# Own steps for the differences of the last two groups' second-layer operands, and a new written order

## The chip, the cores and the metric

The kernel runs on one core of one Trainium2 chip. The time is device microseconds of one execution, from launch to end; three runs of the kernel before gave a median of 918.45 us. The profile is of one more execution, whose own time is given below.

## The reference, cut to what matters

Windowed attention of 4 batches of 8 heads (576 tokens, head size 64, window 128) gives 2304 rows of 512. Two feed-forward layers follow, each 512 to 2048 to 512, and both are computed in full f32 precision:

```
attn = softmax(scale * q @ k.T + bias, masked to the window) @ v
x = attn.transpose(0, 2, 1, 3).reshape(2304, 512)
g = s * relu(x @ w_in1) ** 2 + b;   x = g @ w_out1
h = relu(x @ w_in2);                out = (h * h) @ w_out2
```

## The kernel before

**Precision.** A f32 operand is split in a high part, which ScalarE (ACT) copies to the matmul's type, and a low part, which VectorE (DVE) forms as operand minus high part (`split`, `act_copy`, `dve_sub`). A product is three matmuls: high by high, high by low, low by high.

**Stages.** First attention (steps S, P, T, C, U, X of 40 units, D their loads), with the weights' preparation (l, a, b, c) and the first feed-forward layer of six token blocks beside it (L, G, H, M). Then 32 units of 128 pairs of hidden columns: 8 for the last three token blocks of the first feed-forward layer (group 0) and 8 each for the three groups of 768 tokens of the second one (groups 1 to 3). A unit k makes its hidden values with seven products in place of eight (steps p k.1 to p k.7), with copies m, u, v on ACT and sums j on DVE between them, and squares them (r). In groups 0 and 1 the result is split (h) and multiplied by the second weights directly (F).

**The second product of groups 2 and 3**, around which the change lies. Here the second weights are multiplied by seven products too, over all 8 units of the group: step `X n.e` is one of 56 products of group n. Its index e runs over seven kinds, eight units each: e 0 to 7 is kind 1, then kinds 2, 7, 6, 5, 4 and 3. Each product takes its weights from step `e n.e` (a DMA of 256 KB from a store in DRAM) and its left operand from step `g n.e`. Kinds 1, 2, 5 and 4 split a unit's result as it stands. Kind 7 (e 16 to 23) needs a11 - a21, kind 6 (e 24 to 31) needs a21 + a22 and then that minus a11, both in place, and kind 3 (e 48 to 55) needs a12 - a11 in place. Before, `second_operand` forms them on DVE directly ahead of the split, all in one step. The difference of kind 7 goes to one tile, `r_all` (temp u3). An operand's halves lie in a ring of 6 (group 2) or 10 (group 3) places.

**What sets the order.** `ORDER` is a written list of steps. `InOrder` keeps every engine's instructions in the order in which the steps issue them; there is no scheduler. Each engine works its own list off and waits only on semaphores. All DMAs stand in one queue of SyncE (SP): weights (w, e), stores of prepared weights and sums (d, t, x), inputs (Y), outputs (O), and a DMA that must wait holds all behind it. `CHOICE` says for some steps which of DVE (v) and GpSimd (POOL, g) adds, `UNIT_ENGINES` which of ACT and DVE normalises and copies in an attention unit. Steps of the list in the order of the text: `C n.m.t` copies a bank of a finished kind, `O n.m.t` adds two kinds and stores a part of the output, `R k.i` and `t k.i` split and store sums of second weights that `N k.i` adds, `V` and `T` split and subtract inputs of a group that `Y` loads.

All instructions are recorded at line 29 (the helper), so the names of tiles tell them apart: `q` is a bank of a second product, `px` and `py` those of a unit, `m2...` a place in the weights' memory, `yw...` and `yr` results of units, `sh` and `sl` the one ring place that has tiles of its own.

Of the kernel before, what the change touches and what calls it, by code (L numbers as in the profile page):

```python
# [18 lines left out]
class InOrder:  # L19
# [24 lines left out]
    H13 c21 L15 c20 M12 c22 C10 U10 G14 a23 H14 X10 l30 G15 M13 L16 S11 M14 b23 L17 G16 P11 D13 L18 T11 H15 c23 M15 H16
    C11 G17 l32 a30 G18 U11 H17 X11 H18 L19 G19 b30 L20 S12 M16 L21 k0.1 a32 l31 M17 M18 P12 T12 a31 H19 G20 c30 C12 H20
    L22 l33 G21 b32 U12 X12 L23 G22 H21 S13 L24 M19 a33 b31 M20 M21 H22 P13 l34 b33 T13 G23 C13 c31 a34 M22 H23 U13 L25
    c33 G24 G25 c32 L26 k3.0 D14 L27 H24 M23 H25 X13 D15 S14 G26 G27 M24 l35 b34 L28 L29 P14 k4.1 T14 M25 H26 a35 C14
    H27 c34 k4.0 G29 b35 U14 M26 D16 X14 G28 H28 S15 L30 c35 P15 M27 M28 T15 C15 D17 G30 L31 H29 G31 U15 X15 L32 S16 M29
    H30 H31 D18 G32 L33 P16 T16 M30 D19 C16 H32 G33 M31 M32 H33 S17 U16 L34 P17 T17 X16 G34 C17 M33 L35 H34 S18 U17 M34
    G35 X17 H35 P18 L36 D20 T18 G36 C18 M35 D21 S19 U18 L37 H36 P19 T19 X18 M36 C19 S20 D22 U19 G37 L38 H37 P20 M37 T20  # L50
    G38 X19 C20 L39 S21 U20 H38 G39 H39 L40 P21 M38 G40 L41 M39 D23 H40 T21 G41 L42 X20 H41 C21 k6.0 S22 U21 M40 k0.0
    P22 T22 X21 C22 M41 S23 U22 G42 D24 H42 k7.0 k1.1 L43 P23 T23 X22 M42 C23 S24 G43 H43 k3.1 U23 P24 L44 T24 D25 D26
    C24 X23 M43 k1.0 G44 H44 L45 G45 S25 U24 L46 D27 M44 k5.0 X24 P25 T25 H45 G46 k2.1 C25 H46 D28 L47 n0.0 n0.1 S26 U25
    n0.2 P26 M45 n0.3 G47 n0.4 L48 T26 n0.5 X25 H47 n1.0 k2.0 M46 f0.0 C26 n1.1 G48 M47 n1.3 S27 f0.1 L49 n1.2 H48 E21
    P27 n1.4 D29 U26 T27 n1.5 n2.3 W21 G49 L50 E20 W20 n2.2 X26 C27 S28 U27 n2.1 f1.0 f1.1 n2.0 n2.4 H49 E22 E23 M48
    n2.5 W23 G50 P28 D30 n3.1 n3.0 W22 X27 n3.3 L51 T28 f2.0 f2.1 H50 M49 M50 n3.2 l0.3 n3.4 C28 S29 U28 l0.1 G51 H51
    n3.5 L52 n4.3 P29 T29 G52 k7.1 C29 l0.0 k6.1 X28 f3.0 D31 H52 L53 a0.1 S30 U29 n4.0 n4.1 l0.2 M51 a0.3 G53 f3.1 n4.2
    X29 k5.1 P30 L54 n4.4 n4.5 T30 n5.2 n5.3 a0.0 M52 b0.3 H53 D32 C30 b0.0 x0.3 S31 U30 G54 L55 b0.1 H54 X30 P31 S0.0
    D33 M53 T31 S0.1 c0.0 d0.0 G55 f4.0 D34 L56 c0.1 a0.2 l1.0 H55 f4.1 C31 U31 S32 n5.0 n5.4 b0.2 X31 n5.1 G56 M54 c0.2
    S33 P32 P33 d0.1 n5.5 M55 n6.1 x0.2 T32 d0.2 f5.0 L57 H56 T33 D35 C32 n6.3 U32 S34 n6.0 a1.0 c0.3 G57 C33 n6.2 X32  # L60
    c0.4 H57 l1.1 L58 d0.3 f5.1 U33 S35 X33 M56 P34 P35 n6.4 T34 T35 a1.1 M57 l1.2 c0.5 G58 d0.4 n6.5 C34 U34 b1.0 D36
    l1.3 f6.1 b1.1 n7.1 a1.2 H58 X34 S1.0 C35 L59 U35 S36 S1.1 D37 b1.2 G59 w1.4 L60 X35 M58 P36 T36 H59 c1.0 w2.4 c1.1
    a1.3 S37 D38 d1.0 d1.1 n7.0 D39 f6.0 d0.5 G60 C36 M59 S38 U36 P37 T37 H60 L61 c1.2 d1.2 b1.3 C37 w0.2 S39 P38 T38
    c1.3 d1.3 X36 G61 C38 L62 U38 P39 w2.0 T39 x1.3 c1.4 x1.2 X38 n7.2 n7.3 H61 U37 M60 d1.4 C39 c1.5 X37 U39 d1.5 G62
    X39 Q Y0.0 Y0.1 L63 n7.4 Y0.3 n7.5 M61 w0.0 Y0.2 w0.1 f7.1 H62 f7.0 G63 M62 V0.1 T0.1 H63 T0.2 w0.4 V0.5 M63 E40
    T0.3 p0.1 V0.2 V0.6 p0.2 w0.3 V0.7 m0 p0.6 u0 w1.0 w1.1 j0.0 p0.7 T0.4 r0.0 V0.4 p0.5 v0 h0.0 E41 W40 V0.3 p0.4 j0.2
    w0.5 w1.2 W41 F0.0 F0.2 j0.1 w1.3 w2.2 r0.2 F0.3 p1.1 m1 r0.1 p0.3 p1.6 w2.1 h0.2 j0.3 F0.1 u1 F0.4 h0.1 p1.2 E42
    p1.7 v1 F0.6 j1.0 F0.9 r0.3 p1.5 E43 W43 F0.5 j1.1 w2.5 r1.1 F0.7 p1.4 w1.5 F0.10 r1.0 h0.3 F0.8 F0.11 w4.3 p1.3
    h1.1 j1.2 w2.3 l2.0 F0.12 j1.3 w3.1 p2.1 p2.2 m2 p2.6 h1.0 F1.2 F1.0 u2 F0.14 p2.7 w4.0 j2.0 r1.2 F0.13 v2 p2.5 r1.3
    r2.0 h1.2 F1.3 j2.1 w3.0 r2.1 F1.10 F1.1 p2.4 F1.8 p2.3 j2.2 F1.6 h1.3 F0.15 j2.3 F1.11 w3.3 p3.1 h2.1 m3 p3.2 r2.3  # L70
    w3.2 F1.12 F1.15 h2.0 p3.6 j3.0 p3.5 r2.2 Y1.3 a2.0 F1.7 w4.2 r3.0 u3 h2.2 w4.1 F2.2 h2.3 F1.9 l2.1 p3.7 v3 a2.1
    F2.8 Y1.2 F1.4 p3.4 F1.5 F2.3 b2.0 j3.1 j3.2 F1.13 p3.3 b2.1 j3.3 l2.2 F2.0 F2.6 r3.3 p4.1 r3.2 p4.2 F2.1 F1.14 m4
    p4.6 r3.1 F2.9 F2.10 h3.1 h3.0 u4 p4.7 j4.0 w5.0 p4.5 w3.5 F2.13 F2.4 F2.5 w6.1 F2.11 w4.5 v4 p4.4 S2.0 F2.12 S2.1
    w5.2 h3.2 F2.14 F2.7 c2.1 j4.1 h3.3 c2.0 j4.2 p4.3 p5.1 F3.10 w6.0 j4.3 r4.1 r4.3 w5.3 w3.4 r4.0 F2.15 w5.1 F3.0
    F3.1 m5 d2.1 r4.2 a2.2 F3.9 d2.0 p5.6 h4.0 F3.2 F3.3 u5 p5.2 b2.2 h4.2 w4.4 j5.0 w7.0 F3.14 p5.7 h4.1 F3.11 F3.8
    w7.3 c2.3 v5 p5.4 c2.2 p5.5 j5.2 w6.2 j5.1 r5.2 l2.3 F3.12 x2.2 F3.6 a2.3 h4.3 r5.1 p5.3 F3.7 d2.3 F4.2 F4.8 Y1.0
    b2.3 F3.4 F4.10 j5.3 r5.3 F3.13 F3.15 F4.14 F3.5 h5.2 h5.1 p6.1 F4.9 h5.3 w5.4 p6.2 c2.5 F4.3 W42 F4.12 F4.0 m6 Y1.1
    r5.0 p6.6 h5.0 F4.1 F4.6 u6 j6.0 w5.5 F4.11 w7.1 d2.2 F4.4 w8.0 w6.3 p6.7 F4.13 p6.5 w9.0 F4.7 F4.5 v6 F5.2 j6.1
# [1195 lines left out]
```

## Time and profile before

| | before |
|---|---|
| runs | 918.18, 918.45, 919.23 us |
| profiled execution, its own time | 916.52 us |
| its span, first to last instruction | 914.7 us |
| TensorE (PE) busy | 878.5 us, 96% |
| weight load (PEld) busy | 787.4 us, 86% |
| DVE, ACT, POOL busy | 663.4, 536.7, 167.7 us |
| DMA | 216.83 MB, 70.0% of 16 engines' span |
| granted TensorE clock | 0.996 |

PE is the busy engine nearly everywhere, so what a change is worth is read from the places where PE stands idle: the start, the end of attention, and the second products of groups 2 and 3. In a window's row the first number is its length, then come the busy times of PE, PEld, DVE, ACT and POOL with their instruction counts, the granted clock, the DMA engines' mean busy share and GB/s. A timeline's row has start, length, engine, line, operation, tiles, shapes, the number of instructions merged, and in brackets how long the engine had been idle and what released it.

### The profile page before, as it was taken

The page shows a single profiled execution, that of the slowest core. Times are in us where ns is not written, and L with a number is a line of the kernel's source. Part 1 is how long each engine was busy: PE and PEld are TensorE (multiplying, and loading weights), DVE is VectorE, ACT ScalarE, POOL GpSimd, SP SyncE. Part 2 cuts the span into 40 slices and gives each one's busy share as a digit, 9 for nine tenths or more (in the row PEclk, how much of TensorE's full clock was granted, in tenths as well). Part 3 has the DMA queues.
Part 4 walks back from the last instruction along what each step waited for, and adds up shares of the span by engine and source line. Part 5 has one row for each costly group of instructions (what it writes and reads, how often), then busy time and mean ns, then how long its engine had stood idle before and what let it go on. Part 6 is the DMA issues. An engine that isn't in the chain of part 4 may idle for free.

```text
span 914.7 us, 16299 instructions
## 1 busy us (share of the span) xinstructions
PE 878.5 (96%) x5680; PEld 787.4 (86%) x5680; DVE 663.4 (73%) x1504; ACT 536.7 (59%) x1227; POOL 167.7 (18%) x242
## 2 busy tenths in 40 slices
...
GB/s 344 174 190 99 201 112 195 47 70 219 103 100 242 313 248 271 307 305 316 226 287 355 262 229 198 306 294 261 319 336 349 327 282 252 292 265 229 187 271 98
DMA packets 131378, 216.83 MB, mean 237 GB/s; under 512 B 15840, under 2 KB 74208, under 8 KB 131296
## 3 DMA queue, kind: packets, MB, share of 16 engines
q1 hardware_dynamic: 131296, 215.79, 70.0%
...
## 4 chain that ended last, share of the span: by engine, by line
PE 81%; DVE 9%; ACT 4%; DMA 3%; issue 2%; SPq 1%; POOL 0%; ACTq 0%; DVEq 0%
PE ha L29 14%; PE po L29 14%; PE px L29 13%; PE oa L29 12%; PE py L29 10%; PE q L29 8%; PE s L29 7%; PE u L29 2%; DMA m2wol<-wd 1%; DVE ywoh L29 1%; DVE st L29 1%; DVE m2woh L29 1%; DVE pr_t L29 1%; DMA yf<-xd 1%; DMA st<-w_out 1%
## 5 line engine op out<-in xcount | busy, mean ns | idle before, releaser
L29 POOL TENSOR_TENSOR st<-st 128x256 int32<-128x256 int32 (+1 forms) x123 | 87.2, 729 | 363.8 <-DVE st L29 251.0
L29 ACT ACTIVATE pr<-pr,nd 128x256 f32<-128x256 f32 (+1 forms) x125 | 57.9, 474 | 49.5 <-DVE nd L29 49.5
L29 ACT ACTIVATE st<-st 128x512 int32<-128x512 uint32 (+3 forms) x74 | 62.4, 859 | 5.6 <-DVE st L29 3.4
L29 DVE SCALAR_TENSOR_TENSOR r_all<-r_all,s_sb 128x256 f32<-128x256 f32 (+1 forms) x64 | 43.0, 675 | 24.4 <-ACT r_all L29 23.8
L29 ACT ACTIVATE tr<-tr 128x384 f32<-128x384 f32 x48 | 25.2, 525 | 55.4 <-DVE tr L29 55.3
L29 PE MATMUL oa<-ga,woh 128*128 128x256 f32 x256 | 48.2, 287 | 0.0
L29 ACT ACTIVATE r_all<-ha 128x256 f32<-128x256 f32 (+1 forms) x64 | 31.0, 486 | 24.7 <-PE ha L29 19.2
L29 DVE SCALAR_TENSOR_TENSOR st<-st 128x512 int32<-128x512 int32 (+1 forms) x42 | 37.3, 890 | 11.0 <-ACT st L29 10.4
L29 PEld LDWEIGHTS oa<-ga,woh 128*128 128x128 f32 x256 | 39.7, 191 | 2.2 <-issue 1.8
L29 DVE CUSTOM_DVE_ANT_0 pr<-s,bases 128x256 f32<-128x256 f32 (+1 forms) x96 | 31.7, 385 | 11.3 <-PE s L29 11.3
L29 PE MATMUL ha<-x0h,wih 128*128 128x256 f32 x128 | 38.4, 300 | 0.0
L29 PE MATMUL ha<-x0l,wih 128*128 128x256 f32 x128 | 36.6, 286 | 0.0
L29 PE MATMUL ha<-x0h,wil 128*128 128x256 f32 x128 | 36.6, 286 | 0.0
L29 PE MATMUL oa<-ga,wol 128*128 128x256 f32 x128 | 36.2, 283 | 0.0
L29 POOL TENSOR_TENSOR sph<-wih,wil 128x256 f32<-128x256 f32 x17 | 13.5, 814 | 117.7 <-PE ha L29 117.2
L29 ACT ACTIVATE r_all<-px 128x384 f32<-128x384 f32 x32 | 15.7, 490 | 29.5 <-PE px L29 29.4
L29 PE MATMUL s<-raw 64*128 64x256 f32 (+1 forms) x224 | 30.5, 388 | 0.8 <-DVE x0l L29 0.8
L29 DVE TENSOR_SCALAR st<-st 128x512 int32<-128x512 int32 (+2 forms) x52 | 26.2, 507 | 5.9 <-ACT st L29 5.1
L29 POOL TENSOR_TENSOR sph<-sph 128x256 f32<-128x256 f32 x26 | 22.6, 888 | 33.7 <-DVE spl L29 20.9
L29 PE MATMUL px<-m2xl,m2wil 128*128 128x384 f32 x138 | 27.9, 337 | 0.0
L29 PEld LDWEIGHTS ha<-x0h,wih 128*128 128x128 f32 x128 | 24.9, 195 | 3.5 <-issue 2.5
L29 PE MATMUL ha<-x2h,wih 128*128 128x512 f32 x64 | 26.4, 412 | 0.0
...
## 6 DMA issues: line engine op xcount, KB each, us to landing
...
```

What stands on the lines that cost most here:

```text
L29: ins = op(*args, **kw)
```

## The change

The differences leave `second_operand` and become steps of their own, `q n.e`; the split stays in `g n.e`. Kind 7 now has two tiles in turn, u3 and u4. The written order is new from one end to the other, and so are `CHOICE` and `UNIT_ENGINES`. No product, split or transfer is added or left out. By the two programs POOL has 220 additions in place of 207, DVE 644 in place of 653.

```diff
-    def second_operand(n, e):
+    def parts_of(n, e):
         m, y = SECOND[e // NP], e % NP
         a11, a22, a12, a21 = (result_of(n * NP + y, c) for c in range(4))
+        return m, a11, a22, a12, a21, {1: a11, 2: a12, 7: temp(f"u{3 + y % 2}"), 6: a11, 5: a21, 4: a22, 3: a12}[m]
+
+    def second_difference(n, e):
+        m, a11, a22, a12, a21, src = parts_of(n, e)
         tt = vector.tensor_tensor
-        src = {1: a11, 2: a12, 7: temp("u3"), 6: a11, 5: a21, 4: a22, 3: a12}[m]
         if m == 7:
             tt(src, a11, a21, ALU.subtract)
         elif m == 6:
...
             tt(a11, a21, a11, ALU.subtract)
         elif m == 3:
             tt(a12, a12, a11, ALU.subtract)
-        split(*operand_halves(n, e), src, act_copy, dve_sub)
+
+    def second_operand(n, e):
+        split(*operand_halves(n, e), parts_of(n, e)[-1], act_copy, dve_sub)
...
-            table.update({f"{x}{n}.{e}": lambda y=y, n=n, e=e: y(n, e) for x, y in (("e", load_second), ("g", second_operand), ("X", second_product))})
+            table.update({f"{x}{n}.{e}": lambda y=y, n=n, e=e: y(n, e) for x, y in (("e", load_second), ("q", second_difference), ("g", second_operand), ("X", second_product))})
...
-    N1.1:v N2.1:v N3.0:v N3.1:v N7.1:v S0.1:g S1.1:g S2.0:g S3.0:g S3.1:g S4.0:g b0.0:vg b2.2:vg b3.0:vg b3.1:vg
+    N0.1:v N2.1:v N5.1:v N7.1:v S0.0:g S0.1:g S1.0:g S1.1:g S2.0:g S2.1:g S3.0:g S3.1:g S5.1:g b2.1:vg b2.2:vg
...
+    e2.14 t7.1 e2.15 t7.3 j23.2 t6.3 C2.1.1 r23.2 X2.10 g2.14 g2.13 X2.11 e2.16 g2.16 e2.18 X2.12 X2.13 e2.17 q2.17
```

**DVE in group 2, before.** These rows run from the difference of g2.20 to the low half of g2.25. `r_all` is kind 7's difference, `ywih2`, `ywil2` and others are results of units, and a row that writes `m2...` is the low half of a split.

```order
L29 TENSOR_TENSOR r_all_121<-ywoh0_7286 128x384
L29 TENSOR_TENSOR m2wil1_4703<-r_all_121,m2wil1_4703 128x384
L29 TENSOR_TENSOR ob220_7857<-q220_7699,k2m_7798 128x512
L29 TENSOR_TENSOR r_all_121<-ywol2_7370 128x384
L29 TENSOR_TENSOR m2woh1_4705<-r_all_121,m2woh1_4705 128x384
L29 TENSOR_TENSOR ywih2_7004<-ywih2_7004 128x384 x2
L29 TENSOR_TENSOR m2wih1_4433<-ywih2_7004,m2wih1_4433 128x384
L29 TENSOR_TENSOR r_all_121<-ywol2_7370,ywoh3_7518 128x384
L29 TENSOR_TENSOR m2woh1_4705<-r_all_121,m2woh1_4705 128x384
L29 TENSOR_TENSOR ywil2_7100<-ywil2_7100 128x384
L29 TENSOR_TENSOR ywih2_7004<-ywil2_7100,ywih2_7004 128x384
L29 TENSOR_TENSOR m2wil1_4703<-ywih2_7004,m2wil1_4703 128x384
```

**The same engine and place after**, from the difference q2.19 to the difference q2.22.

```order
L29 TENSOR_TENSOR tu4_7361<-ywoh2_7199,ywoh0_7290 128x384
L29 TENSOR_TENSOR ywih2_6975<-ywih2_6975 128x384 x2
L29 TENSOR_TENSOR m2wih1_4466<-r_all_121,m2wih1_4466 128x384
L29 TENSOR_TENSOR m2wil1_4684<-tu4_7361,m2wil1_4684 128x384
L29 TENSOR_TENSOR r_all_121<-ywoh0_7290 128x384
L29 TENSOR_TENSOR ywoh2_7199<-ywoh2_7199,ywil2_7109 128x384
L29 TENSOR_TENSOR ywil2_7109<-ywoh2_7199,ywil2_7109 128x384
L29 TENSOR_TENSOR m2wil1_4684<-r_all_121,m2wil1_4684 128x384
L29 TENSOR_TENSOR tu4_7361<-ywol2_7347 128x384
L29 TENSOR_TENSOR r_all_121<-ywol2_7347,ywoh3_7527 128x384
```

Before, every low half follows its own difference; now other operands' differences and halves stand between the two, and two tiles hold the differences of kind 7.

**SP in group 2, before.** The loads `m2...<-we` or `<-wd` bring weights of single products (`we22` is that of X2.21, `we41` that of X2.27), `we63<-` is the store t6.3, `out<-` the output stores of O2.2.

```order
L29 DMA m2wol0_4322<-we72_216 128x512
L29 DMA m2wol0_4322<-we62_212 128x512
L29 DMA m2wol1_4678<-we61_211 128x512
L29 DMA m2wol0_4322<-we42_204 128x512
L29 DMA m2wih1_4433<-we32_200 128x512
L29 DMA m2wih3_4650<-we51_207 128x512
L29 DMA m2xl1_4718<-we21_195 128x512
L29 DMA m2wil0_4688<-we12_192 128x512
L29 DMA m2wih1_4433<-we22_196 128x512
L29 DMA m2xl0_4675<-we71_215 128x512
L29 DMA out<-ob222_7850 128x256
L29 DMA we63_213<-m2wil3_4690 128x512
```

**The same queue and place after.**

```order
L29 DMA we63_213<-m2wil3_4698 128x512
L29 DMA m2wol0_4322<-we72_216 128x512
L29 DMA m2wol0_4322<-we52_208 128x512
L29 DMA m2wol0_4322<-we62_212 128x512
L29 DMA m2wol0_4322<-we42_204 128x512
L29 DMA m2wih1_4466<-we22_196 128x512
L29 DMA m2wih1_4466<-we32_200 128x512
L29 DMA m2wih3_4669<-we51_207 128x512
```

The load of X2.21's weights (`we22`) was the ninth, counted from that of X2.16 (`we72`); now it is the fifth. The store t6.3 stands ahead of them and no longer behind an output store.

**SP in group 3, before.** `out<-ob32` are the output stores of O3.2, `we51` the weights of X3.29.

```order
L29 DMA m2wol1_4678<-we62_212 128x512
L29 DMA m2wih3_4650<-we01_187 128x512
L29 DMA m2wil3_4690<-we11_191 128x512
L29 DMA out<-ob320_9148 64x256 x4
L29 DMA out<-ob322_9154 128x256
L29 DMA m2wol0_4322<-we51_207 128x512
L29 DMA m2xl1_4718<-we31_199 128x512
L29 DMA m2wih1_4433<-we00_186 128x512
```

**The same queue and place after.**

```order
L29 DMA m2wil0_4650<-we42_204 128x512
L29 DMA m2wol0_4322<-we41_203 128x512
L29 DMA m2wol0_4322<-we51_207 128x512
L29 DMA m2wol0_4322<-we61_211 128x512
L29 DMA m2wih1_4466<-we00_186 128x512
L29 DMA m2wol1_4693<-we62_212 128x512
L29 DMA out<-ob322_9191 128x256
L29 DMA out<-ob320_9194 64x256 x4
```

The loads for X3.27 to X3.29, X3.31 and X3.32 (`we31` too, further up) stood behind the output stores and now stand ahead of them.

## Rows read from the trace of the kernel before

**Rows 1.** Windows by stage: length, busy PE, PEld, DVE, ACT, POOL, clock, DMA share.
```profile
330.00:412.00 82.00, 76.31 (x474) 61.15 (x473) 65.87 (x169) 57.20 (x143) 21.38 (x39) 1.00 0.88 295
412.00:700.00 288.00, 286.59 (x1544) 264.70 (x1543) 208.86 (x373) 161.86 (x328) 53.12 (x68) 1.00 0.82 287
...
713.40:770.00 56.60, 52.36 (x390) 49.96 (x390) 45.13 (x90) 28.05 (x63) 4.80 (x5) 1.00 0.87 295
770.00:854.40 84.40, 84.40 (x564) 84.40 (x563) 54.89 (x109) 43.08 (x91) 0.00 (x0) 1.00 0.77 252
854.40:882.00 27.60, 24.17 (x188) 22.83 (x188) 19.86 (x40) 9.57 (x20) 0.00 (x0) 1.00 0.66 213
```

**Rows 2.** Timeline of PE: first steps and ends of the two stretches.
```profile
713.05 0.51 PE L29 MATMUL py<-m2xh,m2wol 128*128 128x384 f32 x2
713.39 1.23 PE L29 MATMUL q<-m2wol,m2wih 128*128 128x256 f32 x9
714.46 0.40 PE L29 MATMUL q<-m2wol,m2wil 128*128 128x256 f32 x2
...
767.99 0.52 PE L29 MATMUL q<-m2wil,m2wih 128*128 128x256 f32 x3
...
854.41 1.23 PE L29 MATMUL q<-m2wol,m2wil 128*128 128x256 f32 x9
...
889.87 0.52 PE L29 MATMUL q<-m2wol,m2wil 128*128 128x256 f32 x3
```

**Rows 3.** Waits of PE from 713.4 to 770: total, times, longest.
```profile
PE q L29 <- ACT m2wih L29: 1.8, 1, 1.8
PE q L29 <- ACT m2wil L29: 1.1, 2, 0.6
PE q L29 <- DMA m2wol<-wd: 0.8, 1, 0.8
```

**Rows 4.** Waits of PE from 854.4 to 914.
```profile
PE q L29 <- ACT m2woh L29: 2.3, 2, 1.5
PE q L29 <- ACT m2wil L29: 0.9, 1, 0.9
```

**Rows 5.** Timeline of DVE, ACT, PE around g2.26, and of DVE at 758.
```profile
749.84 0.55 DVE L29 TENSOR_TENSOR ywoh<-ywoh,ywil 128x384 f32<-128x384 f32 x1
...
751.10 0.52 ACT L29 ACTIVATE m2wil<-ywil 128x384 fp32r<-128x384 f32 x1 [1.77 <-DVE ywil L29]
...
751.67 1.57 PE L29 MATMUL q<-m2wih,m2wil 128*128 128x256 f32 x8 [0.60 <-ACT m2wil L29]
752.13 1.14 DVE L29 TENSOR_TENSOR ywoh<-ywoh,ywoh 128x384 f32<-128x384 f32 x2
...
758.33 0.55 DVE L29 TENSOR_TENSOR m2wil<-ywih,m2wil 128x384 fp32r<-128x384 f32 x1
758.80 0.55 DVE L29 TENSOR_TENSOR m2woh<-ywil,m2woh 128x384 fp32r<-128x384 f32 x1
```

**Rows 6.** Timeline of SP and PE: the load for X2.21, and X2.21.
```profile
738.44 0.43 SPq L29 DMA_DIRECT2D m2wih<-we  x1
...
743.17 0.56 DVE L29 TENSOR_TENSOR m2woh<-r_all,m2woh 128x384 fp32r<-128x384 f32 x1 [0.67 <-ACT m2woh L29]
...
745.45 1.31 PE L29 MATMUL q<-m2wih,m2woh 128*128 128x256 f32 x9 [1.82 <-ACT m2wih L29]
```

**Rows 7.** That load alone, asked by its tile: time to landing.
```profile
DMA to landing us min/median/max: 6.9/6.9/6.9
```

**Rows 8.** Timeline of SP: the output stores of O3.2.
```profile
869.75 3.09 SPq L29 DMA_DIRECT2D out<-ob  x5
```

**Rows 9.** Timeline of ACT and PE at the end of attention.
```profile
403.82 0.85 ACT L29 ACTIVATE m2xl<-yf 128x768 fp32r<-128x768 f32 x1 [1.62 <-DMA yf<-xd]
```

**Rows 10.** Waits of PE from 330 to 412.
```profile
PE oa L29 <- DVE ga_63l L29: 2.3, 1, 2.3
```

**Rows 11.** Timeline of POOL from 357 to 368.
```profile
358.20 5.59 POOL L29 TENSOR_TENSOR ewih<-ewih 128x256 int32<-128x256 int32 x5 [4.85 <-DVE ewih L29]
```

More of the change, by code (lines that the diff above doesn't have):

```diff
@@ L44 @@
[L44 to L78, printed above, removed]
@@ new lines @@
+    C12 U12 G20 L22 H19 G21 M19 l33 H20 X12 H21 L23 S13 G22 L24 M20 a33 b31 M21 P13 T13 H22 G23 M22 k2.0 b33 C13 c31 U13
+    L25 H23 X13 G24 L26 M23 l34 c32 G25 a34 D14 H24 H25 b34 l35 L27 c33 G26 S14 L28 G27 P14 M24 L29 T14 k4.0 a35 H26
+    k5.0 M25 c34 D15 C14 G28 b35 U14 H27 X14 L30 S15 M26 G29 H28 c35 D16 H29 D17 P15 G30 M27 M28 L31 T15 k6.0 H30 M29
+    C15 G31 H31 U15 X15 L32 G32 S16 L33 M30 D18 P16 H32 G33 M31 L34 D19 T16 M32 C16 S17 U16 H33 D20 G34 L35 P17 T17 H34
+    M33 C17 k4.1 X16 G35 H35 S18 U17 P18 M34 L36 T18 M35 k7.0 k3.1 G36 C18 L37 X17 H36 S19 U18 M36 D21 P19 T19 G37 L38
@@ new lines @@
+    c0.4 d0.3 f5.1 H57 L58 U33 S35 X33 P34 P35 M56 T34 T35 d0.4 a1.1 c0.5 G58 l1.2 C34 D36 M57 U34 L59 n6.4 l1.3 n6.5
+    f6.1 b1.0 H58 b1.1 X34 n7.1 S1.0 S1.1 C35 D37 a1.2 n7.0 U35 S36 b1.2 G59 w1.4 X35 w2.4 L60 D38 M58 P36 c1.0 H59 T36
+    a1.3 c1.1 G60 d1.0 S37 b1.3 M59 d1.1 D39 f6.0 n7.3 C36 U36 S38 P37 T37 H60 c1.2 L61 d0.5 C37 S39 d1.2 P38 T38 c1.3
+    w0.2 G61 C38 d1.3 L62 w2.0 X36 P39 x1.3 U38 T39 H61 x1.2 c1.4 X38 G62 U37 d1.4 X37 c1.5 C39 M60 d1.5 U39 L63 X39 Q
+    n7.2 H62 Y0.0 M61 Y0.1 G63 n7.4 Y0.3 w0.0 n7.5 M62 Y0.2 w0.1 f7.0 f7.1 V0.1 H63 w0.4 w0.3 T0.1 T0.2 T0.3 M63 V0.5
@@ new lines @@
+    h2.0 w5.2 p3.6 w3.3 F1.9 p3.2 F1.3 r2.2 r2.3 u3 h2.2 F1.14 r2.1 Y1.0 p3.7 w3.5 w5.1 h2.1 F1.6 F2.11 F1.13 j3.0 F2.0
+    a2.1 l2.2 F1.8 p3.5 h2.3 v3 F2.1 p3.4 j3.1 j3.2 F1.7 r3.1 F2.10 p4.1 m4 F1.12 r3.0 F2.2 p4.6 p3.3 b2.1 S2.0 h3.1
+    w3.4 S2.1 F2.3 j3.3 r3.3 F2.4 w4.4 u4 F2.8 W43 F2.5 c2.1 r3.2 c2.0 F2.15 h3.2 p4.7 F2.9 a2.2 w6.1 w6.2 v4 F2.13 p4.2
+    d2.1 w4.5 F2.14 h3.0 j4.0 F2.6 p4.4 j4.2 w7.3 p4.5 r4.2 j4.1 F2.12 F2.7 r4.0 h4.2 F3.0 F3.10 p4.3 F3.2 h3.3 p5.1
+    d2.0 F3.14 h4.0 j4.3 w5.3 r4.1 l2.3 p5.2 Y1.1 c2.3 m5 h4.1 F3.9 p5.6 F3.11 F3.8 F3.3 d2.3 u5 p5.7 r4.3 j5.0 w6.0
@@ new lines @@
+    j7.0 T1.3 F6.0 V1.2 p7.7 v7 w6.5 r7.0 l3.2 F6.6 p7.5 w8.3 p7.4 j7.1 T1.4 w8.1 h6.3 r7.1 w8.4 w8.2 V1.7 F6.11 p7.3
+    j7.2 F6.15 F6.9 p8.1 F6.8 F6.7 w7.4 w9.1 V1.5 F6.1 j7.3 a3.1 F6.12 m8 F6.13 p8.6 F6.10 r7.2 w8.5 F6.4 r7.3 F6.5 b3.1
+    V1.4 u8 p8.7 S3.0 p8.2 h7.0 h7.1 F7.0 w7.5 h7.2 F6.14 F7.1 j8.0 v8 F7.4 F7.2 h7.3 F7.3 F7.6 p8.4 a3.2 F7.5 p8.5
+    w10.0 V1.3 b3.2 S3.1 E80 w10.1 w9.3 r8.0 F7.7 Y2.1 j8.2 E81 j8.1 r8.2 w9.0 W80 F7.9 p9.1 F7.11 Y2.3 F7.8 m9 p8.3
+    r8.1 w9.4 F7.12 h8.1 W81 j8.3 E60 p9.6 F7.15 F7.13 p9.2 Y2.2 W60 h8.0 h8.2 F7.10 w10.3 c3.0 u9 x3.2 r8.3 c3.1 p9.7
@@ new lines @@
+    p11.4 l5.1 l5.0 d4.0 F9.8 b4.3 F10.1 F10.2 j11.2 p12.1 F10.0 x4.3 j11.0 d3.5 a5.1 d3.2 c4.5 p11.5 a5.0 F10.5 b5.1
+    m12 b5.0 j11.1 S5.0 F10.9 p11.3 F10.10 S5.1 l5.2 F10.6 j11.3 F10.11 r11.0 c5.3 c5.2 r11.2 h11.0 c5.1 p12.6 d4.1 u12
+    r11.3 F10.8 c5.0 r11.1 F11.0 l5.3 a5.2 p12.7 p12.2 h11.2 v12 p12.4 l6.1 F11.2 b5.2 F11.6 j12.2 j12.0 F10.7 h11.1
+    d4.4 a5.3 F11.4 r12.2 r12.0 p12.5 b5.3 x5.2 j12.1 r12.1 F11.3 F11.5 c5.4 F11.1 h12.2 F11.8 d4.5 h12.0 F11.7 p13.1
+    h11.3 d5.0 a6.1 F11.11 c5.5 x5.3 T2.1 h12.1 b6.1 m13 p12.3 j12.3 F12.2 p13.6 p13.2 l6.0 F11.9 T2.2 d5.1 F12.5 r12.3
@@ new lines @@
+    F12.1 a6.0 u13 l6.2 h12.3 F12.0 b6.0 d5.5 j13.0 F12.11 S6.0 S6.1 a6.2 p13.7 v13 c6.3 F12.6 p13.5 c6.2 F11.10 d5.4
+    d3.1 b6.2 j13.1 r13.1 c6.0 d5.3 p13.4 F12.7 c6.1 p13.3 r13.0 l6.3 j13.2 F12.3 c6.4 h13.0 F12.9 F12.4 j13.3 F13.0
+    p14.1 F12.8 x6.2 T2.3 h13.1 F12.10 F13.5 a6.3 r13.3 d6.3 d6.0 r13.2 l7.0 m14 b6.3 h13.2 F13.4 h13.3 l7.1 p14.2 a7.0
+    p14.6 c6.5 F13.1 F13.11 u14 b7.0 F13.2 a7.1 b7.1 j14.0 d6.4 F13.3 p14.7 F13.9 v14 p14.5 F13.10 x6.3 Y3.1 S7.0 j14.1
+    p14.4 S7.1 r14.1 p14.3 d6.1 c7.2 F13.8 c7.1 W62 c7.0 F13.6 j14.2 p15.1 j14.3 d5.2 d4.3 r14.0 l7.2 r14.2 h14.1 c7.3
@@ new lines @@
+    h14.0 d6.5 p15.2 d7.1 F13.7 l7.3 a7.2 m15 j15.0 F14.4 p15.6 y0.4 u15 b7.2 r14.3 F14.3 p15.5 d7.0 h14.2 F14.2 h14.3
+    V2.1 d7.3 a7.3 F14.1 d6.2 V2.2 p15.7 c7.4 x7.2 d7.2 F14.5 F14.11 b7.3 v15 W63 d7.4 j15.1 p15.4 x7.3 p15.3 j15.2
+    r15.1 j15.3 r15.0 y0.5 Y3.2 p16.1 p16.2 r15.2 F14.7 w19.0 r15.3 c7.5 h15.1 F14.10 F15.5 h15.3 F15.4 F15.11 V2.7 N0.0
+    F14.8 d7.5 V2.3 R0.0 O1.5 N0.1 F14.9 h15.0 F15.3 F15.9 Y3.3 R0.1 V2.6 F15.10 t0.1 t0.0 F15.1 R0.2 m16 p17.2 O1.4
+    O1.3 t0.2 T2.4 p17.1 R0.3 h15.2 j16.0 y1.4 p16.6 y1.5 F15.7 w20.0 u16 F15.2 p16.7 V2.5 p16.5 t0.3 V2.4 Y3.0 N1.0 v16
@@ new lines @@
+    j16.1 O1.1 p16.4 j16.2 m17 j17.0 F14.0 p16.3 j16.3 p17.6 p18.2 w19.2 R1.1 N1.1 r16.0 w19.3 u17 R1.3 p18.1 R1.2 R1.0
+    p17.7 w19.1 p17.5 F14.6 t1.1 F15.8 y2.4 v17 m18 y2.5 T3.1 t1.0 y3.4 j17.1 j18.0 p17.3 w20.2 w20.1 p18.6 t1.3 j17.3
+    r16.1 u18 r17.0 p17.4 O1.2 r18.0 p18.7 p19.1 j17.2 t1.2 v18 N2.0 N2.1 R2.1 p18.5 p19.2 R2.0 m19 y3.5 r16.3 t2.0
+    F15.0 j18.1 p19.6 R2.2 j19.0 r17.3 F15.6 R2.3 w22.0 p18.3 w21.0 g2.0 p18.4 j18.3 p19.5 t2.1 r17.2 w20.3 N3.0 u19
+    r18.1 R3.0 t2.2 p19.7 t2.3 R3.1 j18.2 N3.1 y4.4 t3.0 y4.5 v19 j19.1 p20.1 t3.1 m20 T3.3 R3.2 p19.4 w21.1 p20.2 R3.3
@@ new lines @@
+    j20.0 t3.2 w21.2 r17.1 j19.2 O1.0 p19.3 y5.4 r18.3 N4.0 r20.0 p20.6 j19.3 p21.1 p21.2 r16.2 u20 p20.7 r19.3 g2.2 m21
+    v20 j21.0 r19.1 p20.5 w22.2 w21.3 j20.1 g2.1 w22.1 N4.1 p20.4 R4.1 p20.3 p21.6 R4.2 j20.2 p22.1 R4.0 w23.0 t4.1
+    j20.3 r18.2 p21.5 r21.0 r19.0 y5.5 u21 R4.3 N5.0 p21.7 p22.2 r19.2 v21 m22 r20.2 j21.1 t3.3 t4.3 j22.0 p21.4 j21.2
+    r20.1 r22.0 w23.2 w22.3 r20.3 p21.3 e2.1 t4.0 p22.6 j21.3 e2.0 p22.5 e2.2 e2.4 p23.2 r21.2 N5.1 g2.5 g2.4 u22 w23.1
+    y6.4 g2.3 p22.7 p23.1 R5.3 R5.1 V3.2 v22 R5.0 y6.5 t5.0 t4.2 j22.1 r21.3 p22.4 T3.2 R5.2 p22.3 m23 e2.3 V3.1 e2.7
@@ new lines @@
+    q2.24 g2.18 g2.19 q2.20 q2.26 g2.20 t7.0 q2.21 e2.23 q2.22 e2.24 X2.17 e2.30 r23.3 r23.1 e2.29 q2.28 X2.18 g2.21
+    X2.19 e2.27 e2.28 m24 g2.22 X2.20 e2.32 X2.21 q2.50 g2.25 g2.24 C2.1.0 e2.34 e2.33 X2.22 q2.23 q2.27 g2.26 O2.2.2
+    g2.28 g2.27 X2.24 X2.25 e2.39 q2.29 O2.2.0 X2.26 g2.32 g2.23 X2.27 g2.33 X2.28 X2.23 e2.35 q2.31 g2.34 X2.32 e2.36
+    X2.33 e2.31 e2.42 g2.29 X2.29 q2.30 e2.47 X2.34 q2.55 g2.30 q2.48 C2.7.0 g2.35 C2.7.1 e2.40 e2.37 X2.30 X2.35 g2.31
+    X2.31 g2.39 e2.38 e2.46 e2.41 g2.36 p24.6 g2.41 e2.43 e2.45 V3.5 g2.37 X2.36 w27.0 X2.37 V3.7 g2.40 g2.38 g2.42
```

139 lines of the change are left out of this document (63 added, 76 removed).

## The prediction

> **What bounds the kernel now.** I read the windows by stage first, because PE is busy 878.5 of 914.7 us and a change can only win where PE is not fed. [Rows 1] show the reader four kinds of stretch. From 412 to 700 us PE lacks 1.41 of 288 us, and from 770 to 854.4 us nothing at all: PE and PEld are both busy 84.40 of 84.40. Three stretches lack something: the end of attention (82 less 76.31, 5.7 us), the second product of group 2 from 713.4 to 770 (56.6 less 52.36, 4.24 us), and that of group 3 from 854.4 to 882 (3.43 us). The clock is 1.00 in all five, so nothing here is owed to it. In group 2 the DMA engines are at 0.87, which will limit what can be had there.
>
> Busy time hides part of the loss, so I counted products instead, from the timeline of PE [rows 2]. The first product of group 2 begins at 713.39 and the next at 714.46: 1.07 us for one that is fed. Up to 767.99, 54.60 us later, stand 36 products and 8 steps of units with six matmuls each, at 0.17 us a matmul (two of them from 713.05 to 713.39). That is 36 x 1.07 + 8 x 1.02 = 38.5 + 8.2 = 46.7 us, so 7.9 us are lost. In group 3, 28 products lie between 854.41 and 889.87: 35.46 less 30.0 leaves 5.5 us lost.
>
> Here the Trainium skill has a rule ("Perfetto Trace Analysis", section "Identifying the Most-Contended Engine"): busy time of matmuls is a poor measure, the share of time in which weights are loaded a better one. By it the two stretches lack 56.6 less 49.96 and 27.6 less 22.83, that is 6.6 and 4.8 us, where PE's own busy time gives 4.2 and 3.4; the trace agrees with the skill in the stretch that is fully fed, where PEld too is 84.40. A sum held to PE's idle time alone could not pass 7.7 us for both, by the rule it could pass 11.
>
> Then I read who ends PE's waits there. In group 2 they are [rows 3] 1.8 us for `m2wih`, twice `m2wil` (1.1 together) and 0.8 us for a load; in group 3 [rows 4] twice `m2woh` (2.3, the longer 1.5) and 0.9 for `m2wil`. All but one name ACT, but two of them are something else, as the timeline tells. X2.21 starts at 745.45 after 1.82 us of waiting, while its operand's low half begins at 743.17 and takes 0.56; its weights were issued by SP at 738.44 [rows 6] and took 6.9 us to land [rows 7], so at 745.3. This wait is a load's. In group 3 the 0.8 us left beside the 1.5 of `m2woh` are X3.28's, whose load stands in SP's queue behind the five output stores that hold it from 869.75 for 3.09 us [rows 8].
>
> **The change, group 2.** No work is added or removed, the 48 differences (64 instructions) only leave the splits and are issued earlier. What that is worth is seen around g2.26 [rows 5]: its first difference runs at 749.84, ACT's copy only starts at 751.10 after 1.77 us on DVE, PE is released at 751.67 after 0.60, and DVE's next work starts at 752.13. So a kind-6 operand holds DVE 749.84 to 752.13 = 2.29 us, while unchained ones follow each other in 0.47 (758.33 to 758.80), and three of these are 1.41. Eight such save 8 x 0.88 = 7.0 us of DVE. A kind-7 low half also waits 0.67 for its copy [rows 6]: eight save 5.4. With two tiles for kind 7, a difference need not wait for the previous low half. These 12.4 us of DVE lie in a stretch of 56.6 us in which DVE is busy 45.13 and so idle 11.5: the waits on the chain are the idle time, and with them gone DVE has about its idle time as lead. X2.21's load goes from the ninth to the fifth place, so its 1.8 is taken too. What stays of the 7.9 us: the load wait of 0.8, and some 1.7 of short ones without a row, which makes 2.5 and a gain of 5.4.
>
> What is late next is the transfers. At share 0.87, the 54.60 us move 47.5 us' worth of full DMA. Were 0.88, the highest of [rows 1], a ceiling, the stretch would need 54.0 us and the gain be 0.6; at 1.00 it would need 47.5 and the bound be 7.1. Part of these transfers can wait for the next stretch (0.77). I take 1.0 us off the 5.4 for loads that land late and keep 4.4; the bounds are 0.6 and 7.1.
>
> **Group 3.** Of the 5.5 us, 2.4 are chained operands (0.9 and 1.5), 0.8 the load behind the stores. DVE has 7.7 us idle (27.6 less 19.86), DMA only 0.66. The stores now follow the loads, and the differences are issued ahead of the splits. I leave 1.2 us for waits that remain: gain 4.3. Bounds: the waits named, 3.2, and all, 5.5.
>
> **End of attention.** S1.0's two additions move from DVE to POOL ahead of b1.2's and of P36's memset, for which T36's transposes wait. Five such additions took 5.59 us [rows 11], so 1.1 each: between 0 and 2.2 us late, and I take 0.7 as the cost, since POOL is busy only 21.38 of 82. It is nearer to the lower end because the memset is not needed as soon as it is issued. M63's wait of 2.3 on H63's low half [rows 10] goes, since H63 is issued earlier. But the products behind it need V0.2's high half, which ACT starts at 403.82 after waiting 1.62 for a load [rows 9], and the load chain is not moved. So I give 0 for it; its bounds are 0 and 2.3.
>
> **The rest** of the order (units' steps F, r, h, weights w, attention) is new as well. PE lacks only 1.41 us from 412 to 700, so at best 1.4 can be won. I take 0, with the loss bounded in the second rival.
>
> **Sum:** 4.4 + 4.3 - 0.7 = 8.0 us from the profiled execution's own 916.52 (span 914.7, 1.8 around it) gives 908.5. That execution is 1.93 below the median of the runs, 918.45, so the forecast against the median is 910.4 us. Its bounds are 0.6 + 3.2 - 2.2 = 1.6 and 7.1 + 5.5 + 2.3 + 1.4 = 16.3, that is 916.9 and 902.2; its own likely range is 906 to 913.
>
> **Rivals.** *First: transfers bind group 2.* At the ceiling of 0.88 its gain is 0.6, group 3 still gives 4.3 and attention takes 0.7: 4.2 us, so 914.3 (range 913 to 916.5). For it: 0.87 in the stretch, a landing of 6.9 us, a wait for a load in [rows 3]. Against it: the stretches on both sides run lower, 0.82 and 0.77, so loads can move.
>
> *Second: the new order makes short waits in the stage of units,* where PE has no slack to give: sums, copies and splits of one unit are written next to products of another, and a step that comes a little late costs PE directly. At 0.5 us a wait (rather less than the 0.6 of [rows 3]) 16 of them, one for each unit of groups 0 and 1, take back all 8.0: 918.4, no change. For it: PE's one row of 1.41 in 288 us shows that the old order fitted closely. Against it: DVE has 79 us and ACT 126 us idle there.
>
> *Third, slower: POOL's additions stop DVE.* The new choice gives POOL 13 additions more, at 1.1 us 14.3 us. If DVE stands while POOL works, at a place where PE waits for DVE (the end of attention, where DVE is busy 65.87 of 82 and has 16 us to spare), all 14.3 reach PE: with the gain of 8.7 of the two groups, 916.5 + 14.3 - 8.7 + 1.9 = 924.0. From 10.5 us exposed on it is slower. For it: DVE, ACT and POOL are all busier there than elsewhere. Against it: the 16 us of idle DVE cover as much. POOL has no work at all from 770 us on, so group 3 cannot be touched.
>
> The Trainium skill speaks for this rival ("SBUF — State Buffer", section "Who interferes with whom"): DVE and GpSimd share a pair of ports under an exclusive lock. No row here compares DVE beside an idle and a busy POOL, so I give it no more than the rival's chance.
>
> **How the numbers follow.** Forecast 0.58, first rival 0.20, second 0.12, third 0.10. No change is 0.2%, 1.8 us, about what a measurement of this kernel can tell. Forecast and first rival are faster: 0.78; same 0.12, slower 0.10. For eight in ten I take 904.5 to 917.0, which cuts the lowest part of the forecast's bounds and leaves out most of the second and all of the third rival.
>
> **What would show it.** In the profile after, from X2.0 to X2.36 should pass about 50.2 us in place of 54.6, and from X3.9 to X3.31 about 31.2 in place of 35.5; PE's waits on `m2woh` and `m2wil` should be gone in both, DVE's idle gaps behind ACT's copies too, and X2.21's load should land before its operand. PE's wait on `ga_63l` should be replaced by one on an input of p0.2, nearly as long. If waits on loads `m2...` stand in place of those on ACT, the first rival holds; if PE lacks 8 us more from 412 to 700, the second; if DVE's additions and subtractions take longer beside POOL and the first product of units starts later than before, the third. The forecast is wrong if the two stretches keep their lengths.

## The result and the profile after

The changed kernel takes 903.91 us (median of 4 runs, 901.14 to 905.10) where before takes 918.32 (917.83 to 919.23): a ratio of 0.9838, 95% interval 0.9814 to 0.9861, so 14.4 us less. The forecast was 910.4 with 904.5 to 917.0. The direction and the two main places were right; the gain is 1.8 times the 8.0 that the sum gave, and the time lies 0.6 below the range. The profiled execution has a span of 902.0 us and took 903.85 itself, 12.7 less than before's. What follows compares these two.

Windows by stage, after. The stretches of groups 2 and 3 start and end at the first matmuls shown in the second fence, the others are as in [rows 1], with the same columns.

```profile
330.00:412.00 82.00, 77.24 (x472) 61.07 (x473) 65.01 (x168) 57.09 (x142) 25.00 (x44) 1.00 0.84 286
412.00:700.00 288.00, 288.00 (x1554) 266.50 (x1553) 210.66 (x369) 164.86 (x332) 57.67 (x75) 1.00 0.83 291
712.50:760.70 48.20, 47.87 (x375) 47.34 (x374) 45.92 (x90) 26.50 (x60) 5.27 (x6) 1.00 0.96 325
762.80:847.10 84.30, 84.30 (x563) 84.29 (x562) 51.88 (x104) 40.40 (x89) 0.00 (x0) 1.00 0.77 256
847.10:873.00 25.90, 25.90 (x218) 25.90 (x217) 23.96 (x50) 12.84 (x29) 0.00 (x0) 1.00 0.83 269
```

Timeline of PE after: the starts of X2.0, X2.36, X3.9 and X3.31. The first two and the third answer to [rows 2].

```profile
712.53 1.23 PE L29 MATMUL q<-m2wol,m2wih 128*128 128x256 f32 x9
...
760.69 1.23 PE L29 MATMUL q<-m2wil,m2wih 128*128 128x256 f32 x9
...
847.12 1.23 PE L29 MATMUL q<-m2wol,m2wil 128*128 128x256 f32 x9
...
873.03 1.24 PE L29 MATMUL q<-m2wol,m2wil 128*128 128x256 f32 x9
```

From X2.0 to X2.36 it is now 48.16 us for the same 36 products and 8 unit steps that took 54.60: 1.5 us over the 46.7 of a fed engine, where 7.9 were lost. Between X3.9 and X3.31 stand 24 products now and not 28, so the 25.91 us are to be held against 24 x 1.07 = 25.7: 0.2 lost, where it was 5.5. The two stretches gave 6.4 and 5.3 us.

All waits of PE after, from 400 us to the end.

```profile
PE py L29 <- ACT m2xl L29: 1.1, 1, 1.1
PE px L29 <- ACT tu L29: 0.6, 1, 0.6
PE py L29 <- DVE m2xl L29: 0.6, 1, 0.6
PE oa L29 <- DVE ga_63l L29: 0.6, 1, 0.6
PE oa L29 <- ACT ga_63h L29: 0.3, 1, 0.3
PE px L29 <- DMA m2wil<-wd: 0.2, 1, 0.2
```

None of the waits of [rows 3] and [rows 4] is left; no `q` stands in the list. The timeline of DVE after, from the difference of g2.20 on, shows why.

```profile
737.35 0.55 DVE L29 TENSOR_TENSOR r_all<-ywoh 128x384 f32<-128x384 f32 x1
737.82 0.55 DVE L29 TENSOR_TENSOR ywoh<-ywoh,ywil 128x384 f32<-128x384 f32 x1
738.40 0.56 DVE L29 TENSOR_TENSOR ywil<-ywoh,ywil 128x384 f32<-128x384 f32 x1
738.88 0.55 DVE L29 TENSOR_TENSOR m2wil<-r_all,m2wil 128x384 fp32r<-128x384 f32 x1
739.34 0.55 DVE L29 TENSOR_TENSOR tu<-ywol 128x384 f32<-128x384 f32 x1
```

The low half at 738.88 takes the difference of 737.35, with the two of a kind-6 operand (q2.26) between them. A step comes every 0.47 us or a little more, and no row has a wait, where [rows 5] had the engine stand until 752.13 for the one operand. DVE is busy 45.92 of 48.20 us: it is now almost as full as PE. The load for X2.21 is issued at 733.65 and lands 5.9 us later, four us ahead of its product (SP's row after, which answers to [rows 6] and [rows 7]):

```profile
733.65 0.38 SPq L29 DMA_DIRECT2D m2wih<-we  x1
```

### The profile page after: what moved, and what is told of

Read it like the earlier page. It is cut to its first block, busy times and chain, and to the rows that moved or that the text cites. A ratio compares the mean times of both kernels' runs of the same rounds, so it can differ in the third digit from the quotient of the medians.

```text
span 902.0 us, 16324 instructions
## 1 busy us (share of the span) xinstructions
PE 878.8 (97%) x5680; PEld 789.1 (87%) x5680; DVE 655.7 (73%) x1493; ACT 536.1 (59%) x1229; POOL 172.3 (19%) x255
## 4 chain that ended last, share of the span: by engine, by line
PE 88%; DMA 4%; ACT 3%; DVE 3%; issue 1%; SPq 1%; ACTq 0%
PE po L29 15%; PE px L29 15%; PE ha L29 13%; PE q L29 12%; PE oa L29 12%; PE py L29 11%; PE s L29 7%; PE u L29 2%; DMA m2wol<-wd 1%; PE s_t L29 1%; ACT st L29 1%; ACT f_3woh L29 1%; DMA rwih<-first 1%; DMA yf<-xd 1%; SPq L29 1%
## 5 line engine op out<-in xcount | busy, mean ns | idle before, releaser
L29 POOL TENSOR_TENSOR sph<-wih,wil 128x256 f32<-128x256 f32 x14 | 10.7, 779 | 119.9 <-PE ha L29 119.7
L29 DVE TENSOR_SCALAR st<-st 128x512 int32<-128x512 int32 (+3 forms) x52 | 27.0, 521 | 5.5 <-ACT st L29 4.7
L29 PE MATMUL ha<-x1h,wih 128*128 128x512 f32 x64 | 26.3, 411 | 0.0
```

Source lines behind the costliest of these rows:

```text
L29: ins = op(*args, **kw)
```

## Experiments

Each was timed beside before. The ratio, not the difference of medians, is to be compared between the four groups of runs (the result above and three later ones), since before itself read 918.32, 916.64, 916.39 and 916.73 us in them.

**One part alone, and both together.** First the code without the order. In `code_only` the differences are own steps, but each directly ahead of its split, and the order is that of before.

```diff
-    X2.15 e2.24 p24.1 r23.3 g2.19 O2.2.2 g2.20
+    X2.15 e2.24 p24.1 r23.3 q2.19 g2.19 O2.2.2 q2.20 g2.20
```

> The order of before with each difference directly ahead of its split, so the instructions of before in their places; only kind 7 has two tiles in turn. Every theory: within 1 us of before, since a difference still stands directly ahead of its split.

Measured: 917.18 us, ratio 1.0006 (0.9996 to 1.0016). The new steps and the second tile are worth nothing by themselves. PE's waits from 690 us on are the old ones; that of X2.21 has its right name here, a load:

```profile
PE q L29 <- DMA m2wih<-we: 2.0, 1, 2.0
PE q L29 <- ACT m2woh L29: 1.5, 1, 1.5
PE q L29 <- ACT m2wil L29: 0.8, 1, 0.8
PE py L29 <- DVE ywoh L29: 0.8, 1, 0.8
PE q L29 <- DMA m2wol<-wd: 0.8, 1, 0.8
```

`pull1` keeps this order and only puts each difference one place of g earlier.

```diff
-    q2.18 g2.18 X2.15 e2.24 p24.1 r23.3 q2.19 g2.19 O2.2.2 q2.20 g2.20
+    q2.19 g2.18 X2.15 e2.24 p24.1 r23.3 q2.20 g2.19 O2.2.2 q2.21 g2.20
```

> The written order and the choices of before; only the differences are own steps, each one place of g ahead of its split, with the two tiles for kind 7. Chain theory (DVE waiting for ACT inside a split costs PE the time in the second products of groups 2 and 3): about 4 to 6 us faster than before, 912 to 914, and DVE's 0.6 to 0.7 us waits for ACT's copies gone there; the two waits for loads stay. Order theory (the gain is the loads' places and the rest of the new order): within 2 us of before, 916.5 to 920.

Measured: 911.24 us, ratio 0.9942 (0.9924 to 0.9960), 5.3 us faster, as the chain theory has it. PE's waits on ACT for an operand's half are all gone. DVE's own waits for ACT's copies, which the expectation had gone too, are still there, but fewer and longer: 6 of up to 2.5 us from 714 to 768 us, where before has 16 of up to 0.7. ACT's longest wait there is one of 3.4 us for PE to free a place, so the two now run ahead of PE. PE's waits from 700 us on are now mostly loads:

```profile
PE q L29 <- DMA m2wol<-we: 2.9, 2, 2.1
PE q L29 <- DMA m2wih<-we: 1.9, 2, 1.3
PE py L29 <- DVE ywol L29: 0.5, 1, 0.5
PE px L29 <- ACT tu L29: 0.3, 1, 0.3
```

The longest is X3.28's, and it is the load that stands behind the stores of O3.2, as the timelines of SP and PE of this run show (the columns as in [rows 6] and [rows 8]). The stores hold the queue for longer than the 3.10 us in which they are issued: ahead of them SP stood 7.6 us for the sum that DVE has to write first (9.3 us in before, 0.5 us in after). The 0.90 us row at 870.45 is two loads, the last of them X3.28's.

```profile
864.90 3.10 SPq L29 DMA_DIRECT2D out<-ob  x5
...
870.45 0.90 SPq L29 DMA_DIRECT2D m2wol<-we  x2
```

```profile
876.78 0.55 PE L29 MATMUL q<-m2wol,m2wil 128*128 128x256 f32 x1 [2.05 <-DMA m2wol<-we]
```

`loads` leaves the differences where they were and moves six DMAs.

```diff
-    e2.17 e2.25 e2.19 ... e2.22 e2.21
+    e2.17 e2.21 e2.25 e2.19 ... e2.22
-    O3.2.0 O3.2.2 ... e3.29 ... e3.27 e3.32 ... e3.30 e3.28
+    e3.29 e3.27 e3.32 e3.30 e3.28 O3.2.0 O3.2.2
```

> The order of before, the differences directly ahead of their splits, and only six DMAs moved: the load of X2.21's weights to behind that of X2.17's, and the loads of X3.27 to X3.30 and X3.32 ahead of O3.2 with its stores. Theory of two interlocked limits (DVE's chain and these loads, each late where the other is mended): 0 to 3 us faster than before, since the chain then holds PE. Order theory, in which the loads are the cause: 4 to 8 us faster.

Measured: 916.44 us, ratio 0.9998 (0.9989 to 1.0008): nothing. The wait of X2.21 is gone, and a few products on, X2.25 waits longer for its operand than X2.21 did for its load (PE's timeline of this run):

```profile
747.74 2.45 PE L29 MATMUL q<-m2wol,m2wil 128*128 128x256 f32 x9 [2.22 <-ACT m2wil L29]
```

`pull1_loads` has both edits.

> Both edits in the order of before: the differences one place of g ahead, and the six loads moved. Two interlocked limits: 9 to 12 us faster than before, so nearly all that the whole new order gave, and clearly more than the sum of the two alone. If something else of the new order matters in groups 2 and 3: no more than 7 us.

Measured: 908.20 us, ratio 0.9910 (0.9896 to 0.9924), 8.2 us faster. Alone the two gave 5.3 and 0.0, together 8.2: the loads are worth 2.9 us once the chain is gone (give or take 2 by the two intervals), and nothing ahead of that. It falls 1 us short of the 9 expected and well short of the whole order. PE's waits from 690 us on:

```profile
PE q L29 <- DMA m2wol<-we: 1.1, 2, 0.7
PE py L29 <- DVE ywoh L29: 1.0, 2, 0.8
PE py L29 <- DVE ywol L29: 0.8, 1, 0.8
PE px L29 <- ACT tu L29: 0.4, 1, 0.4
```

`pull2_loads` puts the differences two places ahead in place of one.

> As pull1_loads, but each difference two places of g ahead of its split. If what pull1_loads lacks against after in groups 2 and 3 (about 5 us) is lead of the differences: 2 to 4 us faster than pull1_loads, so 904 to 906 where before has 916.4. If it lies in the units ahead of X2.0 and in the places of other loads: within 1.5 us of pull1_loads.

Measured: 908.54 us, ratio 0.9905 (0.9888 to 0.9921), the same. What it lacks is not lead of the differences; waits for other loads (1.0, 0.8 and 0.6 us) stand in its list, one of 1.2 for a low half that now comes later, and 0.7 for a result of a unit.

**The reverse.** `glue` is after with each difference put back directly ahead of its split.

```diff
-    q2.19 e2.25 X2.16 q2.24 g2.18 g2.19 q2.20 q2.26 g2.20 t7.0 q2.21
+    e2.25 X2.16 q2.18 g2.18 q2.19 g2.19 q2.20 g2.20 t7.0
```

> The order of after, but each difference moved directly ahead of the split that needs it first. Chain theory: 8 to 12 us slower than after, 912 to 916, PE waiting for m2wil and m2woh in both stretches again. Order theory: within 2 us of after, 902 to 906.

Measured: 924.43 us, ratio 1.0088 (1.0070 to 1.0107), slower than before, and 2.4% above after by the two ratios to before (1.0088 and 0.9849), more than the 8 to 12 us expected. So where the differences stand matters in the new order still more than in the old one. Copies of finished banks (`k2m`, `k3m`) come late here too; that the rest of the order was written for operands without the chain would explain it, but was not tested. PE's waits from 700 us on:

```profile
PE q L29 <- ACT m2woh L29: 4.1, 4, 1.7
PE q L29 <- ACT k2m L29: 3.1, 1, 3.1
PE q L29 <- ACT sh L29: 2.5, 2, 2.1
PE q L29 <- ACT k3m L29: 1.6, 1, 1.6
```

**Which part of the order.** Here one order runs up to a step, and the other's remaining steps follow in their own sequence. Each part brings its own entries of `CHOICE` and `UNIT_ENGINES` along. In `before_then_after` the cut is the first product of unit 20.

> The order of before up to the first product of unit 20 (about 687 us), the order of after for all steps left. If groups 2 and 3 make the gain: 12 to 14 us faster than before, 904 to 906. If the attention and the units before bring part of it, 907 to 912.

Measured: 908.84 us, ratio 0.9910 (0.9893 to 0.9928). It lies in the second band, but the reason given there need not hold: the seam itself holds PE. Of its waits from 660 us on, the first, at 693.79, comes just behind the seam:

```profile
PE px L29 <- ACT ywoh L29: 2.7, 1, 2.7
PE px L29 <- DMA m2wil<-wd: 0.5, 1, 0.5
```

No `q` is in this list, so from X2.0 on it runs as after does. The run doesn't decide on the part ahead.

> The order of after up to the first product of unit 20, the order of before for all steps left, each difference directly ahead of its split. If groups 2 and 3 make the gain: 916 to 919, like before, or 2 us above it by the later start. If the part ahead brings something, 911 to 915.

Measured for `after_then_before`, the opposite: 915.22 us, ratio 0.9984 (0.9971 to 0.9996), 1.4 us faster than before. It lies between the two bands; by the interval the part ahead brings 0.4 to 2.7 us.

> The order of before up to the first product of unit 0 (about 404 us), the order of after for all steps left. If the attention of the new order brings nothing (stage sums of the profiles: 58.5 us lost before and 56.9 after, from 75 to 400 us): within 1.5 us of after. If it brings part of the gain: 2 to 4 us slower than after.

Measured for `before_attention`, cut at the first product of unit 0: 902.90 us, ratio 0.9847 (0.9831 to 0.9862). It equals after. The new order ahead of the units, 772 of the 2511 steps and some 400 us, brings nothing that can be measured, and neither do the new choices of DVE, POOL and ACT in it.

> The order of before for the first 57 us only, then that of after. If after's start is later because of its order: 1 to 2 us faster than after. If the start only differs by the clock granted in a run: within 1 us of after.

Measured for `before_start`: 903.58 us, ratio 0.9850 (0.9833 to 0.9866), again after. The kernel after itself was run once more on the same occasion.

> The kernel after the change once more, beside the three below, so that they are compared on one chip: 0.983 to 0.986 of before, and in the profile the same losses by stage as the first time except at the start, where the first 57 us may differ by 1 to 3 us from run to run with the granted clock.

Measured: 903.19 us, ratio 0.9849 (0.9835 to 0.9864). Neither mixture beats it.

**The additions on POOL.** `pool_as_before` has the order of after, but before's `CHOICE`.

> The order of after with the choice of DVE or POOL of before, so 13 additions more on DVE. If POOL's additions stop DVE: 2 to 8 us faster than after. If they relieve it: 1 to 4 us slower, PE waiting at the end of attention or in the units. If neither matters: within 1 us.

Measured: 908.81 us, ratio 0.9916 (0.9901 to 0.9931), 0.7% or some 6 us slower than after by the ratios of this run and of `after_again`. The windows of this run, end of attention and units, with [rows 1]'s columns:

```profile
330.00:412.00 82.00, 76.36 (x460) 60.05 (x457) 63.55 (x167) 54.60 (x139) 21.88 (x40) 0.98 0.85 281
412.00:700.00 288.00, 286.48 (x1540) 264.26 (x1541) 211.55 (x371) 163.23 (x326) 52.88 (x68) 1.00 0.82 286
```

PE is busy 0.9 and 1.5 us less in these two than after, with POOL busy 3.1 and 4.8 us less (the clock of 0.98 in the first would rather lengthen PE's busy time). By the table below, the run loses nothing from X2.0 on. Its loss shows mostly between the first product of unit 0 and X2.0, which take 312.2 us where after takes 308.3, `after_again` 308.8 and before 309.9. So in the order that was written with them the additions on POOL help in the units. Before has the same choice as this run and is 2.3 us quicker there, so part of the loss looks like a choice that the order was not written for; no run tests that.

**From X2.0 on.** The profiled executions say where the gain lies more sharply than the medians. Below is the span of each, less the start of X2.0 in PE's timeline.

| runs, one execution each | X2.0 to the end, us |
|---|---|
| before, `code_only`, `loads`, `after_then_before` | 201.3, 201.5, 201.4, 201.7 |
| `pull1` | 197.3 |
| `pull1_loads`, `pull2_loads` | 193.0, 194.8 |
| after, `after_again`, `before_start`, `before_attention`, `before_then_after`, `pool_as_before` | 189.5, 189.6, 189.9, 189.7, 189.8, 189.7 |
| `glue` | 212.3 |

The runs of the first row agree within 0.4 us, and so do those of the row of after. So 11.8 of the 12.7 us lie there: 4.0 come with the chain's edit and 4.3 more with the loads; 3.5 stay for other places of the new order.

## Why the prediction was wrong

*Group 2.* Mechanism right, size wrong. The step that failed is "I take 1.0 us off the 5.4 for loads that land late and keep 4.4", with the remainder of 2.5 ahead of it (0.8 for a load, 1.7 for short waits without a row). Measured: a gain of 6.4, a loss of 1.5 left. The share of the DMA engines rose from 0.87 to 0.96 in the shorter stretch, and the only load in PE's list is a unit's, 0.2 us. Its idle time there is 48.20 less 47.87, 0.3 us. The ceiling of 0.88 was only the highest of five stage averages, not a limit: from 690 to 700 us the trace of before itself reads 1.01. So the first rival fell with it. Of the short waits, 1.5 us belong to the chain and have rows in a view that the prediction did not read, the waits of the weight load from 713.4 to 768 us before:

```profile
PEld q L29 <- DVE m2wil L29: 0.9, 3, 0.3
PEld q L29 <- DVE m2woh L29: 0.3, 1, 0.3
PEld q L29 <- DVE m2wih L29: 0.3, 1, 0.3
```

In five products PE had begun with the high half and then stood for the low half that DVE was still writing; after, no such row is left. The wait of 0.8 on a load, which I left standing, went too. It is also absent in `pull1`, where no load has moved, and stands at 0.6 in `pull2_loads`; why it went stays open.

*Group 3.* The step that failed is "I leave 1.2 us for waits that remain: gain 4.3". Measured: 0.2 left, a gain of 5.3, at the upper bound of 5.5. `pull1` shows the step from one wait to the next that the prediction spoke of only in group 2: with the chain gone the load behind the stores cost 2.05 us at X3.28, where the trace of before had 0.8. A wait that stands second in a trace can be shown too small; here what was behind the first was seen only when the first went. In both groups together the prediction kept 4.7 us as lost (2.5, 1.0 and 1.2); 1.7 were (1.5 and 0.2).

*End of attention.* Forecast a loss of 0.7. PE's idle time from 330 to 412 fell from 5.7 to 4.8 us, a gain of 0.9. The wait on `ga_63l` went from 2.3 to 0.6 us and a wait of 1.1 on ACT's half of `m2xl` took its place, as expected of p0.2's input, though not "nearly as long"; the 0.6 for DVE's half stood in before too. The price set for POOL's additions, up to 2.2 us at T36, did not show: no wait of PE on POOL is in the list of that stretch. It was also set high: the five additions of [rows 11] hold one of 2.26 us, while the page of before has 123 others at 0.73 on average. As `before_attention` equals after, none of this adds up to a gain that can be measured.

*The units.* I took 0; PE's 1.41 us of idle time went to 0.00, the best that the bound allowed. The second rival fell with that. `after_then_before`, faster by 1.4, agrees, and `pool_as_before` gives 1.5 back, so in this order the gain goes with the choice of POOL's additions.

*The start* was not in the sum. The first matmul of the ninth attention unit starts at 65.37 us where it was 63.42, 1.9 us later in this pair of executions. `before_start` shows no such cost of the order, and the start differs between executions of one program (last section).

*The sum* of what the profiles show: 6.4 + 5.3 + 0.9 + 1.4 - 1.9 = 12.1 of the 12.7 us; 0.6 is not assigned. Against the 8.0 forecast, 3.0 more come from the two groups and 3.0 more from the stages that I took at -0.7 and 0, less 1.9 at the start. Then I carried before's 1.93 us between profile and median over to the kernel after, whose profiled execution lies at its median (903.85 and 903.91). Without that the forecast would have been 908.5 and the whole range 1.9 lower, with the measured time inside it; the gain would still have been too small. On the later occasion the medians differ by 13.5 us.

*The clock.* The prediction said that nothing was owed to the clock, as all five windows read 1.00. That holds for the execution shown, not for others of the same work: below, runs with waits of 1.5 to 2.2 us show a lower clock behind them. How often that happened in the runs of before that have no trace is open, and what it cost there too.

*The third rival* has the wrong sign: taking POOL's additions back costs some 6 us. DVE was indeed held up beside POOL, but not evenly. Of the 400 subtractions and additions of 128x384 on DVE after, 345 lay beside no POOL addition and took 0.55 us on average. Of the 47 that lay beside one for at least half their time, 27 took 0.54 to 0.56 as well and 20 took 0.62 to 1.15; the 47 average 0.72. The Trainium skill's rule of the shared ports ("SBUF — State Buffer", "Who interferes with whom") has whichever of the two issues first hold the ports for its whole instruction while the other stands. These rows don't contradict it: the longest are 0.6 us longer, about one addition of POOL at its quickest (0.61), and many are not longer at all; which of the two was first, no run here shows. The rival's error is its price. In all DVE lost some 8 us beside POOL (47 times 0.17), spread over the run, where the rival had 14.3 us reach PE in one place.

By the Trainium skill's other rule ("Perfetto Trace Analysis", "Identifying the Most-Contended Engine") weight loads were the better measure: PEld's idle time of 6.6 and 4.8 us in the two stretches gave 11.4, PE's own 7.7. The measured 6.4 and 5.3, together 11.7, agree with the rule: they lie near the first figure and well above the second.

**What is shown and what is not.** Shown by taking the two edits in and out: the chain alone 5.3 us, the loads alone nothing, both 8.2. Shown by the cuts: attention and start bring nothing measurable, and nearly all of the gain lies from X2.0 on. Between `pull1_loads` and after some 5 us remain. By the two traces 3.5 us of them lie from X2.0 on, in the places of other loads and steps, which no run takes apart; 1.6 lie between unit 0 and X2.0 (309.9 and 308.3 us), where `pool_as_before` ties the gain to the choice of POOL's additions.
